# Sliding-window attention and a channel mix on one core: division in two steps, scaled copies that either engine can make, four output buffers, new orders

## The chip, the cores and the metric

The kernel runs on one core of a Trainium2 chip. A core has five engines with instruction streams of their own: TensorE (PE; PEld is its weight load), VectorE (DVE), ScalarE (ACT), GpSimd (POOL) and SyncE (SP), and 16 DMA engines that all of them share. They meet only at semaphores, and each runs its own instructions strictly in the order in which they were written. The metric is the device time of one execution in microseconds (us); the median of three runs of the kernel before is 231.72 us.

## What is computed

Eight batches, eight heads, 576 positions, 64 numbers per head. The attention looks back at most 127 positions and has a bias that grows with the distance; its result, 512 wide, goes through a channel mix with a hidden width of 1024.

```python
scores = scale * np.matmul(q, k.transpose(0, 1, 3, 2))
...
mask = (rel >= 0) & (rel < window)                      # window = 128
scores = np.where(mask, scores + bias[None], -1000000000.0)
...
attn = attn / (np.sum(attn, axis=-1, keepdims=True) + 1e-09)
return np.matmul(attn, v).astype(np.float32)
...
xk = mu_k * x + (1.0 - mu_k) * x_prev                   # x_prev: x one position earlier
xr = mu_r * x + (1.0 - mu_r) * x_prev
k = np.maximum(xk @ w_k, 0.0)
v = k * k @ w_v
r = 1.0 / (1.0 + np.exp(-(xr @ w_r)))
return (r * v).astype(np.float32)
```

## The kernel before

The attention is cut into 32 pieces called `it`, one for each batch `b` and pair of heads `g` (four pairs to a batch). The channel mix is cut into four pairs of batches `P`, each with 1152 columns, and those into units of 256, 384 or 512 columns `c0`. Both are interleaved: while one pair of batches is mixed, the attention of the next ones runs.

A piece of attention goes through these named operations. `score` multiplies k and q on TensorE into two PSUM tiles of the ring `sa` (two buffers). `exp` (ScalarE, L263, two of 1024 columns) and, from batch 1 on, `mask` (VectorE, L271) make the weights. `av` (TensorE, L287) multiplies them with v and a column of ones, so that the sum of the weights stands beside the result. `norm` (VectorE) takes the reciprocal of that sum (L297) and at once multiplies by it (L298). The result is transposed: in batches 0 to 3 by `ot` on TensorE and `xt` on ScalarE (L317), from batch 4 on by a DMA, also `xt`, on SyncE's queue. Then VectorE makes x minus x_prev (`dl`, L330), two scaled copies of that difference (`ma`, L336: one instruction times mu_k, one times mu_r), and adds x_prev to both (`xk`, L347; in batch 0 in parts `xk` and `xr`). In batch 0 `norm`, `dl`, `ma` and `xk` are each cut into a first part of 256 positions and a second of 320.

A unit of the mix is `m1` (TensorE, L359, eight of four matmuls; the first two units have their first three matmuls apart, `m1a`), `rl` (ScalarE, L365, the ReLU into a buffer of the ring `rl`), `kk` (the square, L372 on ScalarE or L374 on VectorE), `m3` and `rs` (the gate, L381 and L387), `m2a` and `m2` (L396, the two halves of the second product), `oo` (VectorE, L402, the product with the gate) and `st` (SyncE, L408, the store). `m1`, `m3`, `m2a`, `ot` and others share the PSUM ring `mm` of four buffers.

From batch 2 on, q and k are brought into matmul shape by VectorE transposes (`tr`, L180, and for the last 64 positions `tl`, L188) and a DMA within the core (`sh`, L196, tile qt, on SyncE's queue). The loads from memory are issued by GpSimd on one queue: `lql` (L124), `lqp` (L108), `lts` (L114, L118), `lvs` (v, L99, L103), and the weights `lwk` (L463), `lwr` and `lwv` (L468). GpSimd also writes constants: `clear0` and `clear` (L480 to L486 and L900: zeros and ones beside v), `ms` (L904, L906). At the start TensorE runs `fill`, matmuls on zeros whose result nobody reads (L201).

What sets the order is a table, `ORDER`, with one list of names for each engine. A planner walks it and writes the instructions; it gives each operation a cost in ns, but with a list for every engine the order within an engine is the list's. `ON_ACT` holds every name of ScalarE's list; an operation that can run on two engines looks itself up there:

```python
act = ("kk", P, c0, fo) in ON_ACT
op(("kk", P, c0, fo), "ACT" if act else "DVE", ...
```

The functions that the change touches, with the profile's line numbers:

Of the kernel before, what the change touches and what calls it, by code (L numbers as in the profile page):

```python
# [8 lines left out]
FP32 = mybir.dt.float32  # L9
# [7 lines left out]
def kernel(  # L17
# [12 lines left out]
    nc = tc.nc  # L30
# [29 lines left out]
    rlp = ctx.enter_context(tc.tile_pool(name="rlp", bufs=4))  # L60
    otp = ctx.enter_context(tc.tile_pool(name="otp", bufs=3))
# [26 lines left out]
    dl_buf = [cst.tile([128, S], BF16, name=f"dl{i}") for i in range(3)]  # L88
    mb_buf = [cst.tile([128, 2, S], BF16, name=f"mb{i}") for i in range(NMB)]
# [201 lines left out]

    def norm(it, t0, t1):
        n = t1 - t0
        a5 = T.pop(("av", it, t0))[:, :, 0:n * W].rearrange("p h (t c) -> p h t c", c=W)
        rc = xup.tile([128, 2, NJ], FP32, tag="rc", name="rc")
        xu = T["xu", it, t0] = xup.tile([128, NJ, 2, D], BF16, tag="xu", name="xu")
        nc.vector.reciprocal(out=rc[:, :, 0:n], in_=a5[:, :, :, D])  # L297
        nc.vector.tensor_tensor(  # L298
            out=xu[:, t0:t1].rearrange("p t h d -> p h t d"), in0=a5[:, :, :, 0:D],
            in1=rc[:, :, 0:n, None].to_broadcast([128, 2, n, D]), op=ALU.mult)  # L300
# [24 lines left out]
    def x_of(it, c0, c1):  # L325
        b, g = divmod(it, G)
        return xt_buf[b % 2][:, g, MB + c0:MB + c1]

    def delta(it, c0=0, c1=S):
        nc.vector.tensor_tensor(out=ring_of("dl", dl_buf, it, c0)[:, c0:c1], in0=x_of(it, c0, c1),  # L330
                                in1=x_of(it, c0 - 1, c1 - 1), op=ALU.subtract)

    def scaled(it, c0=0, c1=S):
        mb, g = ring_of("mb", mb_buf, it, c0), it % G
        for w in range(2):
            nc.vector.tensor_scalar(out=mb[:, w, c0:c1], in0=T["dl", it][:, c0:c1],  # L336
                                    scalar1=mu_sb[:, NPO * w + g:NPO * w + g + 1], scalar2=None,
                                    op0=ALU.mult)
# [145 lines left out]
    def clear_first():  # L484
# [533 lines left out]
```

## Time and profile before

| | |
|---|---|
| median of three runs | 231.72 us (230.85 to 231.91) |
| the profiled execution | 231.78 us, of which the profile's span is 229.9 us |
| TensorE busy | 218.2 us, 95% |
| VectorE busy | 190.4 us, 83% |
| ScalarE busy | 172.7 us, 75% |
| GpSimd busy | 76.4 us, 33% |
| granted TensorE clock | 1.0 over the whole span |

Busy is the time in which an engine executes an instruction; an instruction's time runs from its start to the end of its writes, and two neighbours on one engine can overlap by a little. A busy TensorE is not one at its peak. The chain that ended last runs through TensorE for 74% of the span, DMA for 10%, VectorE for 8%.

### The profile page before, as it was taken

What the parts mean: (1) busy time and instruction counts of PE and PEld (TensorE: products, weight loads), DVE (VectorE), ACT (ScalarE), POOL (GpSimd) and SP (SyncE); (2) the same over time, 40 slices, a digit from 0 to 9 for tenths busy, and PEclk for the clock granted to TensorE, in tenths of its full rate; (3) what the DMA queues carried; (4) which work ended last, traced back from release to release, by engine and by line L of the source; (5) the groups of instructions that cost most, each with busy time, mean ns of one, the idle gap of its engine ahead of it and who ended that gap; (6) DMA issues with size and microseconds to landing.
All of it is one profiled execution on the core that took longest, in us unless ns stands there. A gap on an engine that the chain in (4) does not pass through costs nothing.

```text
span 229.9 us, 5654 instructions
## 1 busy us (share of the span) xinstructions
PE 218.2 (95%) x2226; PEld 128.1 (56%) x2261; DVE 190.4 (83%) x397; ACT 172.7 (75%) x326; POOL 76.4 (33%) x118
## 2 busy tenths in 40 slices
PE   7789989998999999999999999999999999999993
PEld 3446648755766555655566655556565465456541
DVE  7239999999899999999999999999989984761132
ACT  3968999996898997895699896868588668038810
POOL 8989864436565753271139100000000000000000
PEclk9999999999999999999999999999999999999999
DMA  5999999999999999999969996153422124240023
GB/s 112 164 145 157 175 157 201 209 172 182 228 199 185 182 210 199 155 134 208 114 128 112 220 141 146 33 165 128 91 80 74 48 56 120 99 152 26 0 98 130
DMA packets 83225, 31.82 MB, mean 138 GB/s; under 512 B 55032, under 2 KB 78592, under 8 KB 83200
## 3 DMA queue, kind: packets, MB, share of 16 engines
q0 software_dynamic: 61904, 16.52, 79.9%
q1 hardware_dynamic: 21296, 14.95, 25.8%
q8 instruction: 17, 0.28, 0.5%
q14 instruction: 8, 0.07, 0.1%
HBM read 33.56 MB, written 9.44 MB: 187 GB/s over the span
## 4 chain that ended last, share of the span: by engine, by line
PE 74%; DMA 10%; DVE 8%; POOL 3%; issue 1%; ACT 1%; SPq 1%; DVEq 0%; POOLq 0%
PE ps L359 25%; PE pv L396 22%; PE pr L381 11%; PE sa L287 6%; PE sa L242 4%; DMA qt<-qt 4%; DMA out_dram<-ot 3%; DMA vs<-in_v_dram 3%; DVE mb L336 2%; PE xp L306 1%; DVE xm L347 1%; PE sa L229 1%; DVE dl L330 1%; DVE xu L298 1%; PE sa L217 1%
## 5 line engine op out<-in xcount | busy, mean ns | idle before, releaser
L263 ACT ACTIVATE at<-sa 128x1024 bf16<-128x1024 f32 x64 | 64.0, 1031 | 13.7 <-PE sa L247 10.0
L359 PE MATMUL ps<-xm,wk_sb 128*128 128x256 bf16 (+2 forms) x412 | 70.4, 313 | 0.9 <-DVE xm L347 0.6
L396 PE MATMUL pv<-wv_sb,kk 128*128 128x512 bf16 x274 | 66.6, 379 | 0.8 <-issue 0.3
L365 ACT ACTIVATE rl<-ps 128x256 bf16<-128x256 f32 (+2 forms) x104 | 46.1, 474 | 14.0 <-PE ps L359 13.2
L359 PEld LDWEIGHTS <-wk_sb 128*128 128x128 bf16 x416 | 38.9, 98 | 22.5 <-issue 0.2
L396 PEld LDWEIGHTS <-kk 128*128 128x128 bf16 x288 | 26.9, 98 | 28.7
L372 ACT ACTIVATE kk<-rl 128x256 bf16<-128x256 bf16 (+2 forms) x79 | 38.4, 512 | 0.3
L271 DVE TENSOR_TENSOR at<-at,mask 128x1024 bf16<-128x1024 bf16 x56 | 36.9, 680 | 0.9 <-ACT at L263 0.8
L402 DVE SCALAR_TENSOR_TENSOR ot<-rs,pv 128x512 f32<-128x512 bf16 x36 | 24.4, 681 | 14.4 <-PE pv L396 10.5
L381 PE MATMUL pr<-wr_sb,xm 128*128 128x512 bf16 x131 | 35.2, 379 | 0.7
L99 POOL DMA_DIRECT2D vs<-in_v_dram x32 | 28.6, 902 | 20.1 <-PE sa L287 11.1
L387 ACT ACTIVATE rs<-pr 128x512 bf16<-128x512 f32 x36 | 21.3, 605 | 17.3 <-PE pr L381 17.1
L287 PEld LDWEIGHTS <-at 128*128 128x128 bf16 x576 | 21.6, 98 | 6.5 <-issue 1.0
L347 DVE TENSOR_TENSOR xm<-mb,xt 128x1152 bf16<-128x1152 bf16 (+3 forms) x40 | 24.4, 631 | 0.1
L298 DVE TENSOR_TENSOR xu<-sa,rc 128x640 bf16<-128x640 f32 x28 | 23.1, 824 | 1.0
L336 DVE TENSOR_SCALAR mb<-dl,mu_sb 128x576 bf16<-128x576 bf16 (+2 forms) x72 | 23.5, 386 | 0.2
L381 PEld LDWEIGHTS <-xm 128*128 128x128 bf16 x144 | 13.3, 98 | 12.3
L287 PE MATMUL sa<-vs,at 128*128 128x65 bf16 x448 | 18.8, 194 | 0.0
L242 PE MATMUL sa<-qt,kt 32*128 32x256 bf16 (+1 forms) x384 | 15.7, 266 | 1.2 <-DMA qt<-qt 0.7
L124 POOL DMA_DIRECT2D ql<-in_k_dram x15 | 11.7, 778 | 14.7 <-DVE kt L180 9.7
L374 DVE TENSOR_TENSOR kk<-rl 128x256 bf16<-128x256 bf16 (+2 forms) x25 | 8.0, 330 | 8.1 <-ACT rl L365 8.1
L330 DVE TENSOR_TENSOR dl<-xt 128x576 bf16<-128x576 bf16 (+2 forms) x36 | 14.6, 415 | 0.0
(72 smaller groups left out, 208.9 us busy)
## 6 DMA issues: line engine op xcount, KB each, us to landing
out_dram<-ot SPq DMA_DIRECT2D x36, 256.0 KB, 2.5
vs<-in_v_dram POOLq DMA_DIRECT2D x32, 128.0 KB, 8.3
ql<-in_k_dram POOLq DMA_DIRECT2D x15, 256.0 KB, 7.3
ql<-in_q_dram POOLq DMA_DIRECT2D x15, 256.0 KB, 7.6
qt<-qt SPq DMA_DIRECT2D x12, 192.0 KB, 6.8
wk_sb<-in_moe_w_k_dram POOLq DMA_DIRECT2D x2, 512.0 KB, 7.9
wv_sb<-in_moe_w_v_dram POOLq DMA_DIRECT2D x2, 512.0 KB, 13.2
tv<-in_v_dram POOLq DMA_DIRECT2D x8, 64.0 KB, 7.8
```

What stands on the lines that cost most here:

```text
L99: nc.gpsimd.dma_start(out=vs_buf[b % NLD][:, j, :, 0:D], in_=v[b, :, 128 * j:128 * j + 128, :].rearrange("h p d -> p h d"))
L263: nc.scalar.activation(out=to, in_=sa, func=AF.Exp, scale=float(scale))
L271: nc.vector.tensor_tensor(out=a, in0=a, in1=m, op=ALU.mult)
L287: nc.tensor.matmul(pa[:, hl, W * (t - t0):W * (t - t0) + W], lhsT=at[:, lo:lo + 128], rhs=vs[:, u, 2 * g + hl, :] if u < NF else tvb[:, 2 ...
L298: nc.vector.tensor_tensor(out=xu[:, t0:t1].rearrange("p t h d -> p h t d"), in0=a5[:, :, :, 0:D], in1=rc[:, :, 0:n, None].to_broadcast([12 ...
L336: nc.vector.tensor_scalar(out=mb[:, w, c0:c1], in0=T["dl", it][:, c0:c1], scalar1=mu_sb[:, NPO * w + g:NPO * w + g + 1], scalar2=None, op0 ...
L347: nc.vector.tensor_tensor(out=xm_buf[P % 2][:, w0:w1, o:o + c1 - c0], in0=T["mb", it][:, w0:w1, c0:c1], in1=x_of(it, c0 - 1, c1 - 1)[:, No ...
L359: nc.tensor.matmul(ps[:, 0:c1 - c0], lhsT=wk_sb[:, po, 128 * fo:128 * fo + 128], rhs=xk[:, po, c0:c1], start=(po == 0), stop=(po == NPO - 1))
L365: nc.scalar.activation(out=rl[:, 0:c1 - c0], in_=T.pop(("ps", P, c0, fo))[:, 0:c1 - c0], func=AF.Relu, scale=RELU_SCALE)
L372: nc.scalar.activation(out=out_, in_=in_, func=AF.Square)
L381: nc.tensor.matmul(pr, lhsT=T["xr", P][:, po, 128 * c:128 * c + 128], rhs=wr_sb[:, po], start=(po == 0), stop=(po == NPO - 1))
L396: nc.tensor.matmul(pv, lhsT=kk[:, fo, o:o + 128], rhs=wv_sb[:, fo], start=(fo == 0), stop=(fo == NFO - 1))
```

## The change

The reciprocal and the multiplication of `norm` become two operations, `rc` and `norm`, which can stand apart in VectorE's list. The two scaled copies become two operations, `ma` and `mr`, and each runs on ScalarE if its name stands in ScalarE's list, otherwise on VectorE. In batch 0 `mr` is one instruction over all 576 positions. The difference moves from a tile of its own (`dl`) into a third part of the tile `mb`, so that one ring of three holds all three. The ring `rl` has three buffers instead of four, the output ring `ot` four instead of three. All five lists are new.

By the new lists 29 of the 68 scaled copies run on ScalarE (16 `ma`, 13 `mr`; one of them, `ma.2.1`, has 320 columns, the others 576), 61 squares instead of 79 on ScalarE and 43 instead of 25 on VectorE, and five copies `pk` of transposed k on VectorE instead of two. ScalarE's list also names `c.0.1`, a cast of the first k, but that operation has no form for ScalarE and stays on VectorE. The computation is the same, and the lists of TensorE, GpSimd and SyncE hold the same operations as before.

```diff
-    rlp = ctx.enter_context(tc.tile_pool(name="rlp", bufs=4))
-    otp = ctx.enter_context(tc.tile_pool(name="otp", bufs=3))
+    rlp = ctx.enter_context(tc.tile_pool(name="rlp", bufs=3))
+    otp = ctx.enter_context(tc.tile_pool(name="otp", bufs=4))
...
-    dl_buf = [cst.tile([128, S], BF16, name=f"dl{i}") for i in range(3)]
-    mb_buf = [cst.tile([128, 2, S], BF16, name=f"mb{i}") for i in range(NMB)]
+    mb_buf = [cst.tile([128, 3, S], BF16, name=f"mb{i}") for i in range(NMB)]
...
+    def recip(it, t0, t1):
+        n = t1 - t0
+        a5 = T["av", it, t0] = T["av", it, t0][:, :, 0:n * W].rearrange(
+            "p h (t c) -> p h t c", c=W)
+        rc = T["rc", it, t0] = xup.tile([128, 2, NJ], FP32, tag="rc", name="rc")
+        T["xu", it, t0] = xup.tile([128, NJ, 2, D], BF16, tag="xu", name="xu")
+        nc.vector.reciprocal(out=rc[:, :, 0:n], in_=a5[:, :, :, D])
...
-    def scaled(it, c0=0, c1=S):
-        mb, g = ring_of("mb", mb_buf, it, c0), it % G
-        for w in range(2):
-            nc.vector.tensor_scalar(out=mb[:, w, c0:c1], in0=T["dl", it][:, c0:c1],
...
+    def scaled(it, w, act, c0=0, c1=S):
+        mb, i = T["mb", it], NPO * w + it % G
+        mu = mu_sb[:, i:i + 1]
+        if act:
+            nc.scalar.activation(out=mb[:, w, c0:c1], in_=mb[:, 2, c0:c1], func=AF.Copy, scale=mu)
+        else:
+            nc.vector.tensor_scalar(out=mb[:, w, c0:c1], in0=mb[:, 2, c0:c1], scalar1=mu,
+                                    scalar2=None, op0=ALU.mult)
...
-            m2a.0.1 m1.0.256.7 m2.0.0 score.9 m2.0.1 m2a.0.3 m2.0.3 m3.0.5 m1.0.512.0
+            m2a.0.1 m2.0.1 m2a.0.0 m1.0.256.2 m2.0.0 m1.0.512.0 m1.0.512.4 score.10
...
+        def scale_op(name, w, deps, c0=0, c1=S):
+            act = name in ON_ACT
+            op(name, "ACT" if act else "DVE", 280, lambda: scaled(it, w, act, c0, c1), deps, n,
...
-        op(("norm", it), "DVE", 990, lambda: norm(it, 0, NJ), [], n, "xu", uses=[("av", it)])
+        op(("rc", it), "DVE", 130, lambda: recip(it, 0, NJ), [], n, "xu", uses=[("av", it)])
+        op(("norm", it), "DVE", 730, lambda: norm(it, 0, NJ), [], n, uses=[("rc", it), ("av", it)])
...
-        op(("ma", it), "DVE", 560, lambda: scaled(it), [], n, "mb", uses=[("dl", it)])
-        op(("xk", it), "DVE", 670, lambda: mix(it, 0, 2), [], n, uses=[("ma", it)])
+        scale_op(("ma", it), 0, [("dl", it)])
+        scale_op(("mr", it), 1, [("dl", it)])
+        op(("xk", it), "DVE", 670, lambda: mix(it, 0, 2), [("ma", it), ("mr", it)], n,
+           uses=[("dl", it)])
```

The first place is GpSimd's stream at the start, around the loads of batch 0's v (vs_76 and tv_91; ql, xm and kl are parts of q and k). Before:

```order
L906 MEMSET xt_94 128x4x32
L906 MEMSET xt_95 128x4x32
L114 DMA xm_97<-in_k_dram 64x8x64
L114 DMA xm_97<-in_q_dram 64x8x64
L99 DMA vs_76<-in_v_dram 128x8x64 x2
L103 DMA tv_91<-in_v_dram 64x8x64
L118 DMA kl_87<-in_q_dram 32x8x128
L99 DMA vs_76<-in_v_dram 128x8x64 x2
L124 DMA ql_80<-in_q_dram 128x4x256
L124 DMA ql_80<-in_k_dram 128x4x256
```

The same place with the change, where the constants beside the later batches' v (tv_92 to kl_88) now come first:

```order
L123 DMA ql_79<-in_k_dram 128x4x256
L117 DMA kl_87<-in_q_dram 32x8x128
L123 DMA ql_80<-in_q_dram 128x4x256
L487 MEMSET tv_92 64x520
L488 MEMSET tv_92 128x8
L489 MEMSET vs_77 128x32
L487 MEMSET tv_93 64x520
L488 MEMSET tv_93 128x8
L489 MEMSET vs_78 128x32
L926 MEMSET kl_87 32x8x64
L926 MEMSET kl_88 32x8x64
L98 DMA vs_76<-in_v_dram 128x8x64 x4
```

Two loads of batch 1's q and k (ql_80), one of batch 2's tails (kl_87) and all of `clear` have moved ahead of the four main loads of v, which now stand in a row.

The second place is ScalarE's stream where the first unit of the mix begins (at is the attention's weights, rl and kk the hidden layer, xt the transposed result). Before:

```order
L263 ACTIVATE at_83<-sa 128x2x512
L365 ACTIVATE rl<-ps 128x256 x3
L263 ACTIVATE at_84<-sa 128x2x512
L263 ACTIVATE at_83<-sa 128x2x512
L365 ACTIVATE rl<-ps 128x256 x2
L372 ACTIVATE kk<-rl 128x256 x3
L365 ACTIVATE rl<-ps 128x256 x3
```

With the change:

```order
L262 ACTIVATE at_83<-sa 128x2x512
L321 COPY xt_94<-xp 128x320
L342 ACTIVATE mb_100<-mb_100,mu_sb 128x576
L342 ACTIVATE mb_99<-mb_99,mu_sb 128x576
L342 ACTIVATE mb_98<-mb_98,mu_sb 128x576
L342 ACTIVATE mb_99<-mb_99,mu_sb 128x320
L372 ACTIVATE rl<-ps 128x256 x2
L379 ACTIVATE kk<-rl 128x256
```

All `exp` of batch 1 and four scaled copies of batch 0 now stand ahead of the first `rl`.

The third place is VectorE's stream at the divisions of pieces 8 and 9 (batch 2). Before:

```order
L271 TENSOR_TENSOR at_83<-at_83,mask 128x2x512 x2
L297 RECIPROCAL rc<-sa 128x10
L298 TENSOR_TENSOR xu<-sa,rc 128x2x5x64
L297 RECIPROCAL rc<-sa 128x10
L298 TENSOR_TENSOR xu<-sa,rc 128x2x5x64
L188 STREAM_TRANSPOSE qt_90<-kl_88 32x8x2x32
```

With the change:

```order
L187 STREAM_TRANSPOSE qt_90<-kl_88 32x8x2x32
L297 RECIPROCAL rc<-sa 128x10 x2
L301 TENSOR_TENSOR xu<-sa,rc 128x2x5x64
L179 STREAM_TRANSPOSE qt_90<-ql_80 128x4x4x32
L301 TENSOR_TENSOR xu<-sa,rc 128x2x5x64
```

The two reciprocals now stand side by side, and no multiplication follows its own reciprocal at once.

More of the change, by code (lines that the diff above doesn't have):

```diff
@@ L567 @@
[L567 to L570 removed]
+            mask0.4 c.0.1 mask0.2 pq.0 pq.1 mask0.6 exp.0.0 exp.1.0 pq.3 pq.2 mask0.0
+            exp.0.1 exp.1.1 pk.3 exp.2.0 pq.4 pq.5 exp.2.1 xt.0.0 xt.2.0 exp.3.1 exp.3.0
+            xt.1.0 exp.5.0 xt.0.1 exp.4.0 xt.1.1 exp.5.1 pk.7 pq.7 exp.4.1 pq.6 exp.7.0
```

312 lines of the change are left out of this document (158 added, 154 removed).

## The prediction

> **What bounds the kernel now.** I read the page first (busy times), then the busy time by stage, then the waits of TensorE and VectorE.
>
> ```profile
> span 229.9 us, 5654 instructions
> PE 218.2 (95%) x2226; PEld 128.1 (56%) x2261; DVE 190.4 (83%) x397; ACT 172.7 (75%) x326; POOL 76.4 (33%) x118
> PE   7789989998999999999999999999999999999993
> DVE  7239999999899999999999999999989984761132
> 0.00:36.00 36.00, 31.38 (x391) 18.29 (x396) 25.82 (x83) 29.54 (x50) 30.39 (x58) 1.00 1.75 153
> 36.00:192.00 156.00, 153.09 (x1661) 92.31 (x1687) 150.67 (x286) 128.41 (x243) 46.01 (x60) 1.00 1.11 148
> 192.00:216.00 24.00, 23.84 (x133) 13.22 (x135) 10.50 (x24) 12.62 (x33) 0.00 (x0) 1.00 0.20 77
> 216.00:229.90 13.90, 9.85 (x45) 4.31 (x44) 3.44 (x5) 2.12 (x5) 0.00 (x0) 1.00 0.24 94
> ```
>
> In the stage rows the columns after the length are the busy times of PE, PEld, DVE, ACT and POOL. Two engines are full at once: from 36 to 192 us TensorE is idle for 156 − 153.09 = 2.9 us and VectorE for 156 − 150.67 = 5.3 us. From 192 to 216 only TensorE is full (0.2 us idle). Outside lie the head, 36 − 31.38 = 4.6 us idle, and the end, 13.90 − 9.85 = 4.05 us, in which the last product and its store run alone. TensorE's instructions are the same before and after, `fill` too. So the change can win only from those 2.9 us and from the head, however much work it takes from VectorE.
>
> ```profile
> PE tp L154 <- DMA ql<-in_q_dram: 1.3, 2, 0.9
> ...
> PE sa L242 <- DMA qt<-qt: 0.7, 1, 0.7
> PE ps L359 <- DVE xm L347: 0.6, 1, 0.6
> ...
> DVE ot L402 <- PE pv L396: 10.5, 9, 3.4
> ```
>
> TensorE's waits are few and short; only one in the middle is named, 0.7 us for `sh`. The rest of the 2.9 us is small holes. They come where TensorE needs the last thing that VectorE made, so a VectorE that is ahead should close some.
>
> **VectorE's work.** The timeline shows what an instruction really costs, from its start to the next one's:
>
> ```profile
> 37.36 0.21 DVE L297 RECIPROCAL rc<-sa 128x10 f32<-128x10 f32 x1
> 37.61 0.82 DVE L298 TENSOR_TENSOR xu<-sa,rc 128x640 bf16<-128x640 f32 x1
> 38.35 0.21 DVE L297 RECIPROCAL rc<-sa 128x10 f32<-128x10 f32 x1
> ...
> 42.83 0.82 DVE L330 TENSOR_TENSOR dl<-xt 128x576 bf16<-128x576 bf16 x2
> 43.57 0.64 DVE L336 TENSOR_SCALAR mb<-dl,mu_sb 128x576 bf16<-128x576 bf16 x2
> 44.13 0.45 DVE L330 TENSOR_TENSOR dl<-xt 128x576 bf16<-128x576 bf16 x1
> ```
>
> The multiplication (0.82 long) is followed 0.74 us later by an unrelated reciprocal: they overlap by 0.08. The reciprocal (0.21) is followed by its own multiplication only after 0.25, since that needs the result. Standing apart, a reciprocal should cost 0.21 − 0.08 = 0.13, which saves 0.12. Of 36 pairs 8 are still side by side in the new list, so division gives 28 × 0.12 = 3.3 us.
>
> The page "VectorE: DVE Perf Modes" of the Trainium skill says in "The DRAIN you can't avoid" that a next operation does not start until the pipe is empty, with or without semaphores. By that the two steps save nothing. The rows above speak against it for unrelated neighbours (0.74 against 0.82); nothing in the sum rests on the page.
>
> The pair of scaled copies takes 44.13 − 43.57 = 0.56, so 0.28 each. VectorE had 72 such instructions and has 39: 33 × 0.28 = 9.2 us less. What it gains:
>
> ```profile
> L374 DVE TENSOR_TENSOR kk<-rl 128x256 bf16<-128x256 bf16 (+2 forms) x25 | 8.0, 330 | 8.1 <-ACT rl L365 8.1
> L372 ACT ACTIVATE kk<-rl 128x256 bf16<-128x256 bf16 (+2 forms) x79 | 38.4, 512 | 0.3
> L129 DVE COPY qt<-tp 128x512 bf16<-128x512 bf16 x2 | 1.4, 690 | 3.2 <-PE tp L149 1.7 <-PE tp L154 1.5
> L132 ACT COPY qt<-tp 128x512 bf16<-128x512 bf16 x14 | 7.5, 607 | 0.5 <-PE tp L154 0.5
> ```
>
> Eighteen squares at 0.33 − 0.08 make +4.5 us, three `pk` at 0.69 − 0.08 make +1.8 us. **VectorE's sum is −3.3 − 9.2 + 4.5 + 1.8 = −6.2 us**, some 3%.
>
> **ScalarE's work.** No row shows a scaled copy there. The nearest are
>
> ```profile
> L317 ACT COPY xt<-xp 128x576 bf16<-128x576 bf16 x12 | 7.6, 640 | 2.0 <-PE xp L306 2.0
> L372 ACT ACTIVATE kk<-rl 128x512 bf16<-128x512 bf16 x20 | 12.3, 635 | 0.1
> L372 ACT ACTIVATE kk<-rl 128x384 bf16<-128x384 bf16 x23 | 12.0, 533 | 0.1
> 39.97 1.18 ACT L317 COPY xt<-xp 128x576 bf16<-128x576 bf16 x2 [0.16 <-PE xp L306]
> ```
>
> Two `xt` take 1.18, one 0.64, so the next starts after 0.54 and neighbours overlap by 0.10. A square has its source in SBUF, as the scaled copy has; 128 more columns cost it 0.10, so 576 columns would be 0.69 long and cost 0.59. I take 0.58 (between 0.54 and 0.59): 29 × 0.58 = +16.8. Eighteen squares fewer at 0.41 are −7.4, three `pk` at 0.51 are −1.5. **ScalarE: +7.9 us**, 172.7 to about 181 of 230. The planner's cost for the copy on ScalarE is 280 ns, VectorE's price, so its lists were laid out with ScalarE 29 × 0.30 = 8.7 us too light. What hides this is ScalarE's idle time: 156 − 128.41 = 27.6 us between 36 and 192. In the head there is no such cover (29.54 of 36 busy, the rest before its first work and for loads), and there four copies stand ahead of the first `rl`: 2.2 us.
>
> The page "ScalarE: Activation LUTs" of the Trainium skill ("What ACT_TABLE_LOAD costs") says that an operand read per partition, as the scale here is, adds about 93 ns to an ACTIVATE. By it the copies would be 29 × 0.09 = 2.7 us dearer, an estimate; no instruction of this trace has such an operand.
>
> **The middle.** VectorE gets 6.2 us lighter, but the new lists also move what TensorE needs earlier or later. Adding up VectorE's list in step times up to each result that TensorE takes, and TensorE's list up to the taker, the closest places in the new lists are as close as in the old until about 165 us; only after that VectorE comes free, by 4 us. So the relief is not simply time won. The holes shrink between not at all and all 2.9 us; `sh` has more room than before at most scores. I take half: **−1.5 us**.
>
> **The head.** The new lists bring v later.
>
> ```profile
> 7.75 0.83 POOL vs L99
> 8.58 6.69 DMA vs<-in_v_dram
> ...
> 17.98 0.53 POOL L480 MEMSET tv<- 64x520 bf16 x1
> ...
> 20.79 0.75 POOL L463 DMA_DIRECT2D wk_sb<-in_moe_w_k_dram  x1
> ...
> 31.36 0.49 PE L359 MATMUL ps<-xm,wk_sb 128*128 128x256 bf16 x3
> 32.42 0.27 PE L359 MATMUL ps<-xm,wk_sb 128*128 128x256 bf16 x1 [0.56 <-DVE xm L347]
> ...
> L263 ACT ACTIVATE at<-sa 128x1024 bf16<-128x1024 f32 x64 | 64.0, 1031 | 13.7 <-PE sa L247 10.0 <-PE sa L229 2.2 <-PE sa L242 1.1
> ```
>
> Before, the second piece of v is issued at 8.58 and lands at 15.27, and `av` of batch 0 waits for it. With the change `clear` (17.98 to 20.79, 2.8 us) and about two more loads (0.8 each) go first: it is issued near 13.0. At 6.69 it lands at 19.7; as the queue empties in that pause I take about 4.8, hence 17.8. That is 2.5 to 4.4 us later. What covers it: ScalarE has six `exp` (1.03 each) instead of four and two more `pq` to do before its first `xt`, and by its list is not free before about 19.6. From there `exp.6.0`, which `av.4` needs, is 13.1 us of ScalarE's list away: 32.7. VectorE's list from `rc.0.0` (18.1) to `xk.3.0`, which the first whole unit needs, is 14.7 us, with a wait of 0.5 for the first `xt`: 33.3. Before, that point is 32.42. But by then TensorE has done all scores and `av.4`, `av.5` of batch 1 (1.1 us), which it did later before. I take the head as even: **0**, between −0.5 (ScalarE's chain alone) and +2 (v lands at 19.7).
>
> The weights are the second cover there:
>
> ```profile
> L468 POOL DMA_DIRECT2D wv_sb<-in_moe_w_v_dram x2: 740/744/747, 32.6 to 33.3; - x2
> ...
> DMA to landing us min/median/max: 10.1/12.3/14.1
> ```
>
> The last weight lands at 33.3 + 14.1 = 47.4. The new list has the same loads up to there, with `lwk`, `lwr` now behind batch 1's v. Counting back by the spacing of landings (2.5 to 2.9 us for a weight), the first half of w_k lands near 33.6, when the first `m1` is due near 34, the second near 36.4 for 37.5. Each microsecond more is one for TensorE.
>
> **The end** is untouched: same last `m2`, `oo` and store. The fourth output buffer answers no wait of TensorE.
>
> **Sum** against the profiled execution's own 231.78 us: 0 (head) − 1.5 (middle) + 0 (end) = **230.3 us**, and the median 231.72 is as good a start.
>
> **The rivals.**
>
> 1. *The holes stay.* VectorE's idle time is mostly its own waiting for TensorE (10.5 us for `m2`), so both keep waiting for each other wherever the list is tight. For it speaks that the tight places are no looser; against it the lighter VectorE. Middle −0.3: 231.5 us. In this case too falls that division in two steps gives nothing (VectorE only −2.9 us; half the gain, 231.0).
> 2. *Slower: the first loads come late.* One mechanism: v behind `clear`. If the second piece lands after about 18.5, ScalarE's first `xt` and VectorE's first `rc` wait for it and the whole chain to the mix slides, with w_k as late behind it. At 19.7 the head loses 2 us and the later loads keep the queue that much behind for a while, about 1 more, with the middle at −0.3: 234.4; at 19.0 about 233. I put it at 233.5.
> 3. *All holes close* (VectorE ahead everywhere, head −0.5): 231.78 − 2.9 − 0.5 = 228.4 us.
>
> **How the numbers follow.** Forecast 230.3 (229.4 to 231.2): 0.40. Holes stay: 0.20. Late loads: 0.25. All close: 0.15. A measurement here can tell about 0.5% from no change, 1.2 us: faster means under 230.6, slower above 232.9. Of the forecast's 0.40 some 0.26 lie under 230.6; with 0.15 that is 0.41 faster, 0.34 same (0.14 + 0.20), 0.25 slower. The range, 228.2 to 234.0, takes in the third rival's point and the second's up to v at 19.4; outside it I leave 0.07 below and 0.10 above.
>
> **What would show it.** TensorE's idle time from 36 to 192 us should be near 1.4 us instead of 2.9; 2.5 or more is the first rival. VectorE's busy time should be near 184 us and ScalarE's near 181; a scaled copy on ScalarE 0.65 to 0.69 us long (0.75 with the page). Two reciprocals side by side should start 0.13 us apart. The second piece of v should land near 17.8; at 19 or later, with the first `m1` after 35.5, it is the second rival. I am wrong altogether if TensorE's waits name ScalarE in the middle (the copies are then too dear), or if a new wait of over 1 us for a load or for `sh` stands behind 48 us.

## The result and the profile after

In 14 executions each, the changed kernel takes 233.33 us (median, 231.87 to 234.72), the kernel before 231.25 us (230.65 to 232.48). The ratio is 1.0078, with a 95% interval of 1.0051 to 1.0106: slower by 0.8%, 1.8 us. The forecast was 230.3 us. The time lies inside the range (228.2 to 234.0), but on the other side of no change.

The profiled execution took 234.26 us, of which the span is 232.5 us, so it is one of the longer ones. Its page, and its busy times by stage in the same columns as before:

```profile
PE 220.3 (95%) x2229; PEld 128.8 (55%) x2261; DVE 184.7 (79%) x385; ACT 181.1 (78%) x334; POOL 76.8 (33%) x118
0.00:36.00 36.00, 32.38 (x412) 18.64 (x417) 25.24 (x77) 29.46 (x48) 30.61 (x58) 1.00 1.52 150
36.00:192.00 156.00, 151.60 (x1631) 91.44 (x1654) 142.76 (x274) 133.14 (x249) 46.21 (x60) 1.00 1.12 144
192.00:216.00 24.00, 23.84 (x133) 12.74 (x133) 11.99 (x26) 14.04 (x30) 0.00 (x0) 1.00 0.30 102
216.00:232.50 16.50, 12.45 (x63) 5.97 (x62) 4.72 (x9) 4.47 (x11) 0.00 (x0) 0.98 0.25 95
```

VectorE fell from 190.4 to 184.7 us and ScalarE rose from 172.7 to 181.1, close to the forecast (184 and 181). TensorE got nothing of it: from 36 to 192 us it is idle for 156 − 151.60 = 4.4 us, where I had expected 1.4 instead of 2.9. The waits name something that was not there before. First the waits of TensorE and VectorE, then the place in the timeline:

```profile
PE sa L286 <- DMA vs<-in_v_dram: 1.5, 1, 1.5
PE ps L366 <- DVE ot L409: 0.7, 1, 0.7
DVE mb L335 <- DMA xt<-xu: 3.3, 2, 2.1
...
65.99 0.88 POOL L98 DMA_DIRECT2D vs<-in_v_dram  x1 [0.21 <-issue]
...
76.28 0.26 PE L286 MATMUL sa<-vs,at 128*128 128x65 bf16 x3
78.06 0.53 PE L286 MATMUL sa<-vs,at 128*128 128x65 bf16 x12 [1.52 <-DMA vs<-in_v_dram]
```

`av` of piece 12 stops after three matmuls, because a piece of batch 3's v, issued at 65.99, takes 12.0 us to land. The second wait is VectorE's, for a transposing transfer (`xt` of piece 19, SyncE), and it is passed on to TensorE:

```profile
119.22 2.51 SPq L315 DMA_TRANSPOSE xt<-xu  x1
...
DMA to landing us min/median/max: 9.7/9.7/9.7
...
127.51 0.21 DVE L297 RECIPROCAL rc<-sa 128x10 f32<-128x10 f32 x1
128.95 0.46 DVE L335 TENSOR_TENSOR mb<-xt 128x576 bf16<-128x576 bf16 x1 [1.23 <-DMA xt<-xu]
129.33 0.82 DVE L301 TENSOR_TENSOR xu<-sa,rc 128x640 bf16<-128x640 f32 x1
...
130.21 0.41 PE L241 MATMUL sa<-qt,kt 32*128 32x256 bf16 x8 [0.27 <-DVE xu L301]
...
136.18 1.02 PE L366 MATMUL ps<-xm,wk_sb 128*128 128x512 bf16 x4 [0.66 <-DVE ot L409]
```

The transfer is issued at 119.22 and lands 9.7 us later. VectorE stands at the difference that reads it, and the multiplication behind it, the one that gives a PSUM buffer back to the next score, waits too; VectorE has no pause after that until a product `oo` at 135.45, and TensorE waits for this one at 136. (The other of VectorE's two waits for `xt`, 2.1 us, comes at 192 us; `combo` below has it too, 2.0 us at 189, and TensorE has no hole there.)

The first `m1` starts at 34.8 us, 3.5 us later than before (31.36):

```profile
L470 POOL DMA_DIRECT2D wk_sb<-in_moe_w_k_dram x2: 819/826/832, 25.4 to 26.1; - x2
DMA to landing us min/median/max: 8.9/10.1/11.3
...
34.39 0.60 PE L200 MATMUL wm<-zero 128*128 128x512 bf16 x2
34.82 1.47 PE L366 MATMUL ps<-xm,wk_sb 128*128 128x256 bf16 x12
```

The first half of w_k is issued at 25.36 and lands at 34.3; ahead of the first `m1` TensorE runs `fill`.

### The profile page after: what moved, and what is told of

The parts are those of the page before. It is cut to its first block, busy times and chain, and to the rows that moved or that the text cites. A ratio compares the mean times of both kernels' runs of the same rounds, so it can differ in the third digit from the quotient of the medians.

```text
span 232.5 us, 5634 instructions
## 1 busy us (share of the span) xinstructions
PE 220.3 (95%) x2229; PEld 128.8 (55%) x2261; DVE 184.7 (79%) x385; ACT 181.1 (78%) x334; POOL 76.8 (33%) x118
## 4 chain that ended last, share of the span: by engine, by line
PE 57%; DMA 20%; POOL 12%; DVE 7%; issue 2%; POOLq 0%; DVEq 0%
PE pv L403 21%; PE ps L366 18%; DMA vs<-in_v_dram 14%; PE pr L388 10%; DMA wr_sb<-in_moe_w_r_dram 6%; PE sa L286 5%; POOL vs L98 4%; PE sa L241 3%; POOL ql L123 3%; DVE xm L354 2%; POOL xm L113 1%; DVE xu L301 1%; DVE ot L409 1%; DVE kt L179 1%; DVE at L270 1%
## 5 line engine op out<-in xcount | busy, mean ns | idle before, releaser
L379 ACT ACTIVATE kk<-rl 128x256 bf16<-128x256 bf16 (+2 forms) x61 | 29.8, 512 | 0.3
L381 DVE TENSOR_TENSOR kk<-rl 128x256 bf16<-128x256 bf16 (+2 forms) x43 | 13.8, 334 | 14.2 <-ACT rl L372 14.0
L342 ACT ACTIVATE mb<-mb,mu_sb 128x576 bf16<-128x576 bf16 (+1 forms) x29 | 22.1, 794 | 3.5 <-DVE mb L335 3.5
L301 DVE TENSOR_TENSOR xu<-sa,rc 128x640 bf16<-128x640 f32 x28 | 22.6, 817 | 0.3
L335 DVE TENSOR_TENSOR mb<-xt 128x576 bf16<-128x576 bf16 (+2 forms) x36 | 14.9, 416 | 4.1 <-DMA xt<-xu 3.3
L344 DVE TENSOR_SCALAR mb<-mb,mu_sb 128x576 bf16<-128x576 bf16 (+2 forms) x39 | 13.8, 361 | 0.2
```

Of the source, the lines that this page charges most:

```text
L301: nc.vector.tensor_tensor(out=T["xu", it, t0][:, t0:t1].rearrange("p t h d -> p h t d"), in0=T.pop(("av", it, t0))[:, :, :, 0:D], in1=T.po ...
L379: nc.scalar.activation(out=out_, in_=in_, func=AF.Square)
```

## The experiments

Ratios are to the kernel before, run on the same chip in the same rounds, with 95% intervals. The groups of runs were on different chips, so two runs are compared by their ratios, and a difference between two of them in us is the difference of the ratios times 231. "Lag", where an expectation speaks of it, is the clock less the TensorE work done by then, added up from the trace's weight loads with 512 columns as 0.216 us (their usual spacing in these traces). Lists are cut to the places that change.

### Does the new code or the new order cost the time?

`old_orders`: the new code with the old lists and the old sizes of the rings `rl` and `ot`.

```diff
 # VectorE: norm of the kernel before, as two operations
-norm.9 norm.8 tl.3.0
+rc.9 norm.9 rc.8 norm.8 tl.3.0
...
-    rlp = ctx.enter_context(tc.tile_pool(name="rlp", bufs=3))
-    otp = ctx.enter_context(tc.tile_pool(name="otp", bufs=4))
+    rlp = ctx.enter_context(tc.tile_pool(name="rlp", bufs=4))
+    otp = ctx.enter_context(tc.tile_pool(name="otp", bufs=3))
```

> The code of the changed kernel (division and copies as operations of their own, the difference in the third part of one ring) with the lists of the kernel before: reciprocal right ahead of its multiplication, both copies side by side on VectorE, rings rl 4 and ot 3 as before; two differences (10 and 27) stand two or three places later, since one ring of three now holds what two held. If the loss comes from the new lists, this is the kernel before: ratio 0.998 to 1.002. If it comes from the new code (the merged ring, the split), ratio 1.005 or more.

Ratio 0.9998 (0.9969 to 1.0028). The new operations and the merged ring `mb` cost nothing that the interval shows. What costs is the new lists or the sizes of `rl` and `ot`, which this run set back too; `combo` below keeps the new sizes and has no loss, so the sizes alone don't make it. This profile also has every matmul on record, which that of before has not:

```profile
PE 221.3 (97%) x2261; PEld 128.3 (56%) x2261; DVE 189.7 (83%) x393; ACT 172.3 (75%) x326; POOL 76.5 (33%) x118
0.00:36.00 36.00, 33.59 (x429) 19.87 (x430) 26.10 (x81) 30.57 (x53) 30.99 (x59) 1.00 1.62 158
36.00:192.00 156.00, 154.72 (x1663) 91.39 (x1660) 149.76 (x284) 127.63 (x241) 45.52 (x60) 1.00 1.11 149
...
216.00:229.00 13.00, 8.98 (x42) 3.87 (x40) 3.44 (x5) 1.23 (x3) 0.00 (x0) 0.96 0.26 101
```

The last row is the end. In the old order TensorE is idle for 156 − 154.72 = 1.28 us in the middle, not 2.9. The trace of before has 2226 of 2261 matmuls, so of the 2.9 that I read some 1.6 us were most likely matmuls that it had lost.

### The two late transfers

`v3_early` swaps two loads, so that the late piece of v goes nine places earlier in GpSimd's list. `v3_v6_early` also takes two pieces of batch 6 out of the burst of loads beside the transfer of piece 19. `v3_norm_first` is `v3_early` with the multiplication of piece 21 ahead of the waiting difference. `v3_xt19` is `v3_early` with the transfer of piece 19 issued earlier.

```diff
 # GpSimd (v3_early)
-lvs.4.1 lvs.3.2 lql.4.0.0 lvs.3.0 lvs.3.3 lts.4.1 lql.5.0.0 lvs.3.4 lvs.4.0 lvs.3.1
+lvs.3.1 lvs.3.2 lql.4.0.0 lvs.3.0 lvs.3.3 lts.4.1 lql.5.0.0 lvs.3.4 lvs.4.0 lvs.4.1
 # GpSimd (v3_v6_early, besides)
-lvs.5.2 lvs.7.1 lvs.7.0 lvs.6.2 lvs.7.3 lvs.6.3
+lvs.5.2 lvs.6.2 lvs.6.3 lvs.7.1 lvs.7.0 lvs.7.3
 # VectorE (v3_norm_first, besides v3_early)
-rc.21 dl.19 norm.21
+rc.21 norm.21 dl.19
 # SyncE (v3_xt19, besides v3_early)
-xt.17 sh.6.0 st.1.0 st.1.3 xt.19
+xt.17 xt.19 sh.6.0 st.1.0 st.1.3
```

> The changed kernel; only two loads of GpSimd's list change places: the piece of batch 3's v that av.12 waits for (it landed at 78.0 us in the profile) goes where a piece of batch 4's v stood (landed at 64.6). Theory L (late transfers cost the time): TensorE's wait of 1.5 us for v at 76.5 us goes and the kernel gains 1 to 1.6 us, ratio to the kernel before 1.001 to 1.004 instead of 1.008. Theory O (the new lists are tight in any case; TensorE waits for the next thing instead): the hole is filled by another wait within 15 us, ratio 1.006 to 1.010.

> As the run before, and two pieces of batch 6's v go ahead of the burst of loads at 117 to 123 us, so that the transposing transfer issued at 119.2 us (9.7 us to landing) has five loads beside it, not eight. Theory L: its landing takes 6 to 8 us, VectorE's wait of 1.2 us for it goes, TensorE's holes at 129.7 and 135.2 us (0.5 and 0.8 us) shrink, another 0.5 to 1.2 us gained, ratio 0.997 to 1.001. Theory O: the same as the run before within 0.3 us.

> The changed kernel with the early piece of batch 3's v (as v3_early), and in VectorE's list the multiplication of piece 21 goes ahead of the difference of piece 19, which waits for a transposing transfer (9 to 11 us to landing in all three traces). Theory Q (VectorE's queue: the norm behind the waiting difference holds back the PSUM buffer that the next score needs, 0.5 to 1.8 us at 128 to 130 us): that wait of TensorE goes, 0.5 to 1.5 us less than v3_early, ratio 0.999 to 1.004. Rival: the scaled copies and the xk of piece 19 are what m1 needs in the end, so the hole only moves to 134: ratio 1.005 to 1.009.

> The changed kernel with the early piece of batch 3's v (as v3_early), and in SyncE's list the transposing transfer of piece 19 goes ahead of one transfer within the core and two stores of 256 KB, so that it is issued about 1 us earlier, before most of the burst of loads at 117.5 to 123 us. Theory X (that transfer, 9 to 11 us to landing, holds the difference, the copies and the xk of piece 19, and with them m1, at 128 to 135 us): it lands 2 us earlier or more, TensorE's holes at 128 to 135 us (0.65 us in v3_early's profile, 1.3 to 2 us in the others) go, ratio 0.001 to 0.005 below v3_early's 1.007. Rival: it lands no earlier, since what it shares with the loads is not the order of issue; ratio as v3_early.

`v3_early`: 1.0071 (1.0038 to 1.0103). The wait at 76 us is gone from the profile, and the time hardly moves. In this execution another load was late instead, batch 1's v in the head, although nothing ahead of it was changed, and the first `m1` started 0.9 us later than in the profile of the changed kernel:

```profile
33.27 0.63 PE L286 MATMUL sa<-vs,at 128*128 128x65 bf16 x15 [0.95 <-DMA vs<-in_v_dram]
...
35.68 1.47 PE L366 MATMUL ps<-xm,wk_sb 128*128 128x256 bf16 x12
```

Behind 76 us the swap also uncovers a later wait, as theory O said, in part: at 86 to 87 us a score waits for VectorE's transpose of k (0.17 us here, 0.57 in `v3_norm_first`, 0.70 in `v3_xt19`), and in the last two the transpose itself waits for a load of k.

With the order of v unchanged the same wait is 1.52 us in the profile of the changed kernel, but 0.75 in `head_start` and 0.17 in `clear_late`: how late that piece is differs from profile to profile, which also fits the wide spread of the times. `v3_v6_early`: 1.0101 (1.0068 to 1.0135), not better, so two loads fewer beside the transfer of piece 19 did not help. `v3_norm_first`: 1.0069 (1.0034 to 1.0103), as the rival said:

```profile
126.66 0.82 DVE L301 TENSOR_TENSOR xu<-sa,rc 128x640 bf16<-128x640 f32 x1
129.02 0.46 DVE L335 TENSOR_TENSOR mb<-xt 128x576 bf16<-128x576 bf16 x1 [1.54 <-DMA xt<-xu]
129.40 1.28 DVE L409 SCALAR_TENSOR_TENSOR ot<-rs,pv 128x512 f32<-128x512 bf16 x2
...
130.13 0.60 PE L366 MATMUL ps<-xm,wk_sb 128*128 128x256 bf16 x4 [0.93 <-DVE ot L409]
```

The multiplication is early now; the two products behind the waiting difference are late instead, and TensorE waits 0.93 us for them. `v3_xt19` removes VectorE's wait itself:

```profile
L315 SPq DMA_TRANSPOSE xt<-xu x1: 1204/1204/1204, 117.3 to 117.3; - x1
DMA to landing us min/median/max: 6.5/6.5/6.5
```

The wait at 129 us is gone, and between 88 and 192 us TensorE has no hole that exceeds 0.15 us. Ratio 1.0055 (1.0032 to 1.0077): 0.16% under `v3_early`, which the intervals don't tell from nothing.

### The head

`clear_late` moves the constants behind the loads of batch 1's q and k, `clear_late_wk` also puts the first half of w_k ahead of batch 1's v, `head_start` is meant to make the first `exp` earlier.

```diff
 # GpSimd (clear_late)
-lql.1.0.0 clear lvs.0.0
+lql.1.0.0 lvs.0.0
...
-lql.1.1.0 lvs.1.1
+lql.1.1.0 clear lvs.1.1
 # GpSimd (clear_late_wk, besides)
-clear lvs.1.1 lql.2.0.0 lvs.1.4 lvs.1.3 lvs.1.2 lvs.1.0 lwk.0
+clear lwk.0 lvs.1.1 lql.2.0.0 lvs.1.4 lvs.1.3 lvs.1.2 lvs.1.0
 # GpSimd, VectorE, TensorE (head_start)
-lqp.1.1 place
+place lqp.1.1
-sid dper
+dper sid
-tail.0 score.0.0
+score.0.0 tail.0
```

> The changed kernel; in GpSimd's list only the constants (clear, 2.8 us) move, from ahead of batch 0's v to behind the last load of batch 1's q and k, so that the queue of loads does not empty at 12 us. Theory H (the head loses because the first half of w_k lands late: the first m1 started 0.5 to 0.7 us after its landing in all four traces with the new lists, at 34.8 to 36.2 us): w_k lands 1 to 2 us earlier, the first m1 by as much, ratio 1.002 to 1.005. Rival (ScalarE, over 99% busy from 24 to 36 us, sets the first m1): first m1 not before 34.5 although w_k is there at 33.5 or earlier, ratio 1.006 to 1.010.

> As the run before, and the first half of w_k also goes ahead of batch 1's v, where it stood before the change. It lands near 27 us, so no m1 waits for it. Theory H: the first m1 starts at 32 to 33.5 us, when the mix input of the first units is ready, and TensorE's lag at 48 us falls from 12.3 to 12.9 us to 11 to 11.5: ratio 0.999 to 1.004. Rival: batch 1's v, now one weight (2.7 us) later, holds av.4 and everything behind it, or ScalarE does: first m1 after 34.5, ratio 1.006 or more.

> The changed kernel with the start of the lists nearer the old one: GpSimd's distance table first (before a load), VectorE's scaled identities behind the distances, the tail transposes of TensorE behind the first score. Theory A (ScalarE sets the head: its first exp started at 10.9 us instead of 8.7, and it is full from 12 to 36 us with four scaled copies more to do): the first exp starts about 1 us earlier, TensorE's lag at 48 us falls by 0.6 to 1 us, ratio 1.003 to 1.006. Rival (the loads set it: first m1 0.5 us after the first half of w_k): first m1 stays at 34.8 or later, ratio 1.006 to 1.010.

`clear_late`: 1.0055 (1.0032 to 1.0078); w_k lands at 33.2 us and the first `m1` starts at 34.21, only 0.6 us earlier. `clear_late_wk`: 1.0088 (1.0054 to 1.0123), and theory H falls in its simple form: w_k is there at 27.4 us, yet the first `m1` starts later still, and batch 1's v is late for the `av` that stand ahead of it. That w_k ahead of it made v late isn't shown: `v3_early` has the same wait with w_k in its place.

```profile
32.06 0.33 PE L310 MATMUL xp<-ident,xu 128*128 128x128 bf16 x3
33.29 0.61 PE L286 MATMUL sa<-vs,at 128*128 128x65 bf16 x15 [0.89 <-DMA vs<-in_v_dram]
...
35.68 1.04 PE L366 MATMUL ps<-xm,wk_sb 128*128 128x256 bf16 x8
```

`head_start`: 1.0105 (1.0070 to 1.0140); the first `exp` came at 10.83 instead of 10.91 us, so the edit did not do what it was for and the run tells nothing of ScalarE.

`old_head` and `new_head` join the lists of both kernels at about 47 us: old head and new rest, and the other way round.

```diff
 # new_head, TensorE's list: 104 operations of the new, then the old order of what is left
 m1.0.512.0 m1.0.512.4 score.10
-m3.0.4 m1.0.512.7 m1.0.512.6
+m2a.0.3 m2.0.3 m3.0.5
```

> The changed code; each engine's list begins as in the kernel before (up to about 47 us: 110 of TensorE's operations and what they need) and goes on in the new order, with eleven operations near the seam moved so that no engine waits for itself; rings rl 4, ot 3. Theory S (the head of the new lists costs about 1.5 us, because it puts batch 1's v, the first half of w_k and four more scaled copies all ahead of the first rl; the middle gives nothing back on the mean): 1.2 to 1.8 us less than the changed kernel, ratio 1.000 to 1.003. Rival M (the head is as good, the loss lies in the middle): ratio 1.006 to 1.010.

> The mirror image: each engine's list begins in the new order (104 of TensorE's operations, to about 50 us) and goes on as in the kernel before, one operation moved at the seam; rings rl 4, ot 3. Theory S: slower than the kernel before by 1.2 to 1.8 us, ratio 1.005 to 1.008, first m1 after 34 us. Rival M: ratio 0.998 to 1.002.

`new_head`: 1.0151 (1.0114 to 1.0187), more than theory S said; its first `m1` starts at 34.5 us, and behind the seam there are new holes (0.2 us at 57.4 and 0.6 at 59.6). `old_head`: 1.0407 (1.0366 to 1.0447). Here the seam spoils the answer:

```profile
0.00:48.00 48.00, 43.92 (x555) 27.47 (x563) 37.34 (x104) 40.64 (x79) 35.06 (x64) 1.00 1.58 167
48.00:84.00 36.00, 29.63 (x340) 18.26 (x343) 31.16 (x57) 26.68 (x49) 22.05 (x30) 0.95 1.75 180
```

TensorE is idle for 6.4 us between 48 and 84, where eleven operations had to be moved. Neither join measures the head alone.

### The parts of the change, one at a time

`copies_dve` takes ScalarE's 29 copies back to VectorE in the new lists; `old_act_copies` brings 28 copies to ScalarE in the old ones. `old_rc_apart` lets one operation stand between reciprocal and multiplication in the old lists (33 of 36 pairs); `rc_adjacent` joins them again in the new ones. `fixed_scale` has a constant as the factor and so leaves out mu_k and mu_r in these copies.

```diff
 # copies_dve, VectorE
-dl.6 mr.7 ma.7
+dl.6 ma.6 mr.7 ma.7
 # old_rc_apart, VectorE
-rc.9 norm.9 rc.8 norm.8
+rc.9 rc.8 norm.9 norm.8
...
-rc.12 norm.12 tr.4.0.1
+rc.12 tr.4.0.1 norm.12
 # rc_adjacent, VectorE
-rc.17 rc.18 norm.17 norm.18
+rc.17 norm.17 rc.18 norm.18
 # fixed_scale
-func=AF.Copy, scale=mu)
+func=AF.Copy, scale=0.5)
```

> The changed kernel with its 29 scaled copies of ScalarE moved back to VectorE, each right behind the difference that it scales; everything else in the new order. If a lighter VectorE is worth time in these lists, VectorE's extra 29 x 0.28 = 8.1 us opens holes at TensorE: slower by 1 to 4 us, ratio 1.012 to 1.025. If VectorE was not what TensorE waits for, ratio 1.006 to 1.010. If ScalarE's copies (0.80 us long by the trace, not 0.65 to 0.69) are themselves what is late, faster: ratio under 1.005.

> The lists of the kernel before with the changed code; of each piece from batch 1 on, one of the two scaled copies (28 in all) goes to ScalarE, next to what ScalarE did when the difference was ready. This is the move of the copies alone, from 38 us on: VectorE 28 x 0.28 = 7.8 us lighter, ScalarE 28 x 0.67 = 18.8 us heavier. If VectorE is what TensorE's small holes wait for, 0.5 to 2 us faster than old_orders, ratio 0.991 to 0.998. If both wait for each other, ratio 0.998 to 1.002. If ScalarE's in-order list holds back rl or exp, slower: 1.003 or more.

> The lists of the kernel before with the changed code (as old_orders); 33 of the 36 multiplications stand one place later, so that another operation lies between each and its reciprocal. This is the division in two steps alone. If a reciprocal standing apart saves 0.12 us, VectorE's busy time falls by about 4 us (33 x 0.12) against old_orders, and reciprocals side by side start 0.13 us apart. On the time: if a lighter VectorE closes holes of TensorE, 0.3 to 1.5 us faster than old_orders, ratio 0.994 to 0.998; if not, ratio 0.998 to 1.002.

> The changed kernel with each reciprocal moved back to stand right ahead of its multiplication (28 moved): the new lists without division in two steps. VectorE's busy time rises by 28 x 0.08 = 2.2 us (its time by 28 x 0.12 = 3.4 us). If VectorE's time counts in the new lists, slower than the changed kernel by 0.5 to 3 us, ratio 1.010 to 1.020. If it does not, ratio 1.006 to 1.010.

> The changed kernel with a constant in place of mu as the factor of ScalarE's 29 scaled copies (so it leaves out mu there); all else as it is. If reading the factor per partition is what makes such a copy 0.80 us long, it becomes 0.67 to 0.71 us long, near the 0.69 that I had from the squares, and ScalarE's busy time falls by 2.5 to 3.5 us. If the form of the copy itself costs it, it stays at 0.80.

`copies_dve`: 1.0246 (1.0194 to 1.0298), 3.9 us slower than the changed kernel: in the new lists these copies belong on ScalarE. `old_act_copies`: 1.0158 (1.0123 to 1.0192), 3.7 us slower than `old_orders`, although VectorE's busy time fell from 189.7 to 183.4 us: TensorE's waits now name ScalarE's `exp` (0.9 us) and its `kk`, `rl` and `rs`. `old_rc_apart`: 1.0125 (1.0092 to 1.0159), 2.9 us slower than `old_orders`, with VectorE less busy (187.6 us). Its waits and timeline say why:

```profile
PE sa L241 <- DVE xu L301: 1.5, 3, 0.9
PE xp L310 <- DVE xu L301: 1.0, 2, 0.7
...
83.48 0.21 DVE L297 RECIPROCAL rc<-sa 128x10 f32<-128x10 f32 x1
83.61 1.03 DVE L179 STREAM_TRANSPOSE kt<-ql 128x512 f32<-128x512 f32 x1
84.50 0.80 DVE L301 TENSOR_TENSOR xu<-sa,rc 128x640 bf16<-128x640 f32 x1
...
85.35 0.41 PE L241 MATMUL sa<-qt,kt 32*128 32x256 bf16 x8 [0.88 <-DVE xu L301]
```

The transpose that now stands between the two halves makes the multiplication 0.77 us later (84.50 instead of 83.48 + 0.25 = 83.73), and with it the PSUM buffer that the next score needs. The split saves 0.12 us of VectorE's time and can cost TensorE 0.9 us. `rc_adjacent`: 1.0105 (1.0060 to 1.0150), too wide to tell from the changed kernel. Of `fixed_scale` there is one execution; its copies (second line) against those of the changed kernel:

```profile
L342 ACT ACTIVATE mb<-mb,mu_sb 128x576 bf16<-128x576 bf16 x28 | 21.6, 803 | 3.5 <-DVE mb L335 3.5
...
L342 ACT ACTIVATE mb<-mb 128x576 bf16<-128x576 bf16 x28 | 19.2, 713 | 3.4 <-DVE mb L335 3.4
```

The factor per partition costs 803 − 713 = 90 ns, and the copy without it is 0.02 us longer than the 0.69 that I had from the squares.

### All repairs at once

`combo` is the changed kernel with `clear_late`, `head_start`, `v3_early` and the earlier transfer of piece 19. `combo_rc_adj` joins the reciprocals again in it; `combo_head_dve` takes the four copies ahead of the first `rl` back to VectorE.

```diff
 # combo_head_dve, ScalarE and VectorE
-xt.3.1 mr.1 mr.2 mr.3 ma.2.1 rl.0.0.1
+xt.3.1 rl.0.0.1
-norm.5 norm.4 xr.1 mask.7.0 rc.6 xr.3 xr.2
+norm.5 norm.4 mr.1 xr.1 mask.7.0 rc.6 mr.3 xr.3 mr.2 xr.2
```

> The changed kernel with all repairs that looked right: constants behind the loads (clear_late), the early start (head_start), batch 3's v (v3_early) and the early transfer of piece 19 (v3_xt19). If the causes are separate and add up: head 0.6 to 1.5 us, v 0 to 1.6 us, piece 19 0.5 to 1.5 us better than the changed kernel, ratio 0.995 to 1.001. If each repair only uncovers the next wait: ratio 1.003 to 1.008.

> The repaired version (combo) with each reciprocal right ahead of its multiplication (28 moved): what division in two steps is worth where the waits for transfers are closed. VectorE's busy time plus 2 us, its time plus 3.4 us. If the forecast of the middle was right (a VectorE with less to do closes holes), slower than combo by 0.5 to 1.5 us, ratio 1.002 to 1.008. If what counts is when the division is done and not how long VectorE is busy, the same as combo: ratio 0.998 to 1.002.

> The repaired version (combo) with the four scaled copies that stand ahead of the first rl on ScalarE back on VectorE, each right ahead of the xr or xk that needs it: ScalarE 4 x 0.67 = 2.7 us lighter between 33.7 and 36.4 us, VectorE 4 x 0.28 = 1.1 us heavier between 36 and 40. Theory A2 (what is left of the loss, the head, is these copies on a full ScalarE: the first rl starts at 36.4 us instead of 34.0): first rl at 34 to 35 us, 0.5 to 1.5 us faster than combo, ratio 0.994 to 0.999. Rival (VectorE is as full there, or the landing of w_r near 39.6 us sets the end of the head): ratio 0.999 to 1.003.

`combo`: 1.0005 (0.9984 to 1.0026). The whole loss is gone, 0.73% or 1.7 us, and the spread is smaller too (12 executions from 230.14 to 231.72 us). Its stages, every matmul on record:

```profile
PE 221.3 (97%) x2261; PEld 128.6 (56%) x2261; DVE 183.3 (80%) x385; ACT 181.4 (79%) x334; POOL 76.6 (33%) x118
0.00:36.00 36.00, 32.31 (x417) 18.45 (x418) 24.81 (x77) 29.86 (x48) 30.42 (x58) 1.00 1.60 152
36.00:192.00 156.00, 155.96 (x1672) 93.08 (x1670) 144.85 (x282) 135.87 (x254) 46.20 (x60) 1.00 1.09 147
...
216.00:229.00 13.00, 9.00 (x42) 3.89 (x40) 3.80 (x6) 1.60 (x4) 0.00 (x0) 0.96 0.31 121
```

Set against `old_orders`, whose span is also 229.0 us and whose trace is also complete, TensorE's idle time is (between 192 and 216 us both are at 24.00 of 24):

| us idle | 0 to 36 | 36 to 192 | 192 to the end | span |
|---|---|---|---|---|
| `old_orders` | 2.41 | 1.28 | 4.02 | 229.0 |
| `combo` | 3.69 | 0.04 | 4.00 | 229.0 |

By these two profiles, where no transfer is late, the new lists win all of the middle (1.24 us) and lose as much in the head (1.28 us). Of the 1.28 us that the old order loses in the middle, 0.80 is one hole at 55.47 us. The trace names ScalarE there, but its `rl` had ended at 54.71. What came last for the score was `sh`, issued behind VectorE's transpose at 47.41 and landed at 55.34 (the profile of before names `sh` for the same wait). In `combo` that transpose ends 2 us earlier and `sh` lands at 52.77. The old order's other two holes there, 0.30 and 0.18 us, are waits for VectorE.

Where the changed kernel loses can be read by TensorE's weight loads, which are all on record in these traces and stand in nearly the same order. The table sets the start of the n-th load against that of the n-th in `combo`; the columns are times in `combo`:

| us behind `combo` | at 40 | 74 | 78 | 120 | 134 | end |
|---|---|---|---|---|---|---|
| changed kernel | 0.5 | 0.4 | 2.1 | 2.2 | 3.5 | 3.5 |
| `head_start` | 0.6 | 0.6 | 1.5 | 1.6 | 3.0 | 3.0 |
| `clear_late` | 0.3 | 0.2 | 0.6 | 0.7 | 1.4 | 1.4 |
| `v3_early` | 1.1 | 1.1 | 1.1 | 1.4 | 2.0 | 2.0 |
| `v3_xt19` | 0.1 | 0.1 | 0.1 | 0.7 | 0.7 | 0.7 |

In its profiled execution the changed kernel loses 1.7 us where batch 3's v is late (74 to 78) and 1.3 us where piece 19's transfer is (120 to 134), and next to nothing between. Each loss is gone where its repair was made.

`combo_rc_adj`: 1.0054 (1.0031 to 1.0076), 1.1 us slower than `combo` (by both intervals 0.4 to 1.8): here the division in two steps does win. TensorE's idle time in the middle is 0.90 us instead of 0.04, and in the head 36 − 31.59 = 4.41 instead of 3.69. `combo_head_dve`: 1.0067 (1.0035 to 1.0098), 1.4 us slower: theory A2 falls, the four copies are better on ScalarE than on VectorE. Where this loss lies is not shown.

## Why the prediction was wrong

- **VectorE's and ScalarE's work: the totals right, ScalarE's in part by luck.** An operation behind a reciprocal that it doesn't need starts 0.13 us after it, as forecast, here in the changed kernel:

```profile
37.59 0.21 DVE L297 RECIPROCAL rc<-sa 128x10 f32<-128x10 f32 x1
37.72 0.77 DVE L354 TENSOR_TENSOR xm<-mb,xt 128x576 bf16<-128x576 bf16 x2
```

 By the sentence of the Trainium skill that the prediction weighed ("VectorE: DVE Perf Modes", "The DRAIN you can't avoid") nothing would be saved; the trace agrees instead with the exception that the same section adds, that a next operation that is not held starts earlier. The scaled copy was mis-sized: 0.80 us, not 0.65 to 0.69. From its start to the next one's it takes 0.67 us, not 0.58, which makes 29 × 0.09 = 2.6 us more; that ScalarE's total still came out at 181 is luck, since the rest of its work came out some 2 us less than the sum had it. The rule of the Trainium skill that I had put aside ("ScalarE: Activation LUTs", "What ACT_TABLE_LOAD costs": about 93 ns for an operand per partition) holds here, with 90 ns in `fixed_scale`. It didn't decide the time: the copies on ScalarE are worth 3.9 us in these lists, and TensorE's waits in the middle don't name ScalarE.
- **The middle: the step that failed.** "I take half: −1.5 us" rested on VectorE alone. That a VectorE that is ahead closes holes is borne out: with the transfers in time, the middle wins 1.24 us in `combo`, and joining the reciprocals again costs 1.1 us, in the profiles about half of it in the middle. How much of the 1.24 comes from less work and how much from the new order isn't separated; the largest part is the `sh` that is issued earlier. But of transfers behind 48 us I had looked at `sh` only, "`sh` has more room than before at most scores". The loads of v and the transposing transfers, which the new lists also move against their takers, I took as in time. Two were not: batch 3's v (1.5 us of TensorE's time in the profile) and the transfer of piece 19 (waits of 0.27 us at 130.2 and 0.66 at 136.2, and what shows only as slack between matmuls, 1.3 us in all against `combo`). I had named just this as what would make the prediction wrong, a new wait of over 1 us for a load, and had no rival with a price for it. In numbers: −1.5 us was forecast and 1.8 us slower was measured. Of the 3.3 us between, late transfers make 1.7 (the changed kernel against `combo`), the head 1.3, and the middle 0.3 (1.24 won instead of 1.5).
- **The bound was read from a trace with gaps.** The 2.9 us of idle time in the middle were 1.3. The forecast took half of a room that was less than half as large; that 1.5 lies near the 1.24 won is luck. The third rival, all 2.9 us closed, had no such room. The waits of the kernel before also held one of 0.3 us for VectorE (a score waiting for `xu`), which the prediction passed over when it called the 0.7 us for `sh` the only one in the middle.
- **The head: "0", mis-sized.** It costs 1.28 us in `combo` against `old_orders`. v came as computed (second piece at 18.2 us, forecast 17.8), but the halves of w_k landed at 34.3 and 37.4 us, where I had 33.6 and 36.4, and I let that pass as even. The four copies ahead of the first `rl` took 2.65 us of ScalarE (33.76 to 36.41), not 2.2. What binds the head isn't settled: with w_k at 27.4 us, v of batch 1 was late; with w_k at 33.2 the first `m1` gained 0.6 us in `clear_late`, with w_k at 33.5 nothing in `combo` (34.75); with the first copies on VectorE the time was longer. That the new order asks for batch 1's v and w_k within the same few microseconds fits this, but no run had both in time, so it is not shown.
- **The rivals.** The second (v behind `clear`) has the right sign, and its 233.5 us lies next to the measured 233.33 by luck: neither of its signs came (v's second piece at 18.2 us and not 19, the first `m1` at 34.8 and not after 35.5), moving `clear` back won 0.23%, which the intervals don't tell from nothing, and of the 3.5 us that the profiled execution is behind `combo`, 3.0 are lost behind 74 us. The first, the holes stay, fits the sign that I had set for it (2.5 us or more idle from 36 to 192), but not what happened: the old holes closed and others opened. (The second's upper sum, 231.78 + 2 + 1 − 0.3, is 234.5 and not 234.4.)
- **The end** was untouched, as said: 4.02 and 4.00 us idle.

That late transfers make the loss is shown by `combo` as a whole and by the places in its table. Its other edit, `head_start`, is not about a transfer, but its three swaps stand at the very start of the lists, and the first `m1` comes no earlier in `combo` than in the changed kernel (34.75 against 34.82). The single repairs won 0.07% (v), 0.16% more (piece 19) and 0.23% (`clear`) with intervals of about ±0.3%, so how the 0.73% divides between them on the mean isn't known.

## What to carry to other kernels

When lists are reordered, check every transfer against its taker over the whole run, in the order of its queue; here a VectorE with less to do earned nothing while two transfers were late. A split of an operation that hands a buffer back saves the engine's time and can delay the hand-over, so try it in the order in which it is to stand: such a split cost 2.9 us in the old lists and won 1.1 us in the repaired new ones. Before idle time is taken as the room that can be won, compare the number of matmuls on record with that of weight loads.

## What was not expected of the hardware

In these profiles the time that piece 19's transposing transfer takes goes with what SyncE issued just ahead of it. It took 9.7 us behind a transfer within the core and two stores of 256 KB, 6.5 and 7.1 us ahead of them (`v3_xt19`, `combo`), and 7.4 us in the kernel before; later ones, with no loads beside them, took 2.6. The earlier place also issues it 0.5 us sooner into GpSimd's burst of five loads of v (1.2 us behind the first of them instead of 1.7). Two loads fewer in that burst (`v3_v6_early`) did not make the kernel faster. Beyond that run the loads were not varied with SyncE's list held, so what the transfer shares with the stores or with the loads is not shown.
